# A decode attention and FFN kernel on one Trainium2 core: tiles of four KV heads in 32 KB runs, expanded scores with an additive mask, full-tile transposes of the probabilities, FFN and output weights loaded last

## The chip, the cores and the metric

The kernel runs on one core of one Trainium2 chip (trn2). The metric is the device time of one execution in microseconds (us), as the median of several. Every place in time named below ("190.3 us") is a place in a profile, counted from the start of its span.

The engines are PE (matmul), DVE (vector), ACT (scalar), POOL (GpSimd) and SP, which here only issues transfers. The data moves on 16 DMA engines. A run counts as slow when it is over 1.5% above the fastest of the same kernel.

## The reference

Four decode tokens, one in each of four batches, go through grouped-query attention over the last 4096 places of a KV cache, and through a gated FFN. A scalar gate mixes the two results.

```python
# B = 4, D = 512, Hq = 32 query heads, Hkv = 8 KV heads, Dh = 128, F = 1792, window W = 4096; all bf16
g = sigmoid((x * gate_w).sum(-1, keepdims=True))
q = (x @ wq).reshape(B, 1, 32, 128).transpose(0, 2, 1, 3)
k, v = k_cache[:, :, -W:, :], v_cache[:, :, -W:, :]      # each KV head serves 4 query heads
p = softmax(q @ k.T * Dh ** -0.5)
a = (p @ v).reshape(B, 1, 4096) @ wo
b = (relu(x @ W_gate) * (x @ W_up)) @ W_down
out = g * a + (1 - g) * b                                # [4, 1, 512]
```

The K window and the V window are 33.6 MB each, wq and wo 4.2 MB each, the three FFN matrices 1.8 MB each: 81 MB, and each byte is read once.

## The kernel before

It works on "pairs": two KV heads of one batch, 2 MB of K and 2 MB of V. Two pairs make a set; there are eight sets, and a set is scored together. The names in the code are those of the steps:

- `KT`: K comes in with rows on the partitions (16 KB runs in HBM). PE transposes it as fp32 words that hold two bf16 each, and DVE and ACT copy the result back from PSUM, the memory that PE writes its results to.
- `SC`: scores. Each head has 8 rows in a group of 32 partitions, so 32 of 128 partitions of a score tile carry data. `SW` shares the maxima between partitions.
- `EXP`: two exponentials a set, of 64 partitions each, write the even and the odd columns of `pe`.
- `PT`: PE multiplies `pe` with a selection matrix, which gives transposed probabilities. `PV`: 64 small matmuls a pair apply V. `NORM` divides by the row sums (`RS`), `OQ` rearranges the result for the output matmul.
- `GU`, `HT`, `FFN`, `T2`: the FFN. `WO`: the 32 matmuls with wo. `FIN`: the mix.

```python
KSLOTS, VSLOTS = 4, 5            # slots of 2 MB; gate, up and down weights pass through V slots 2, 3, 4
VLAG, VPIECES = 3, 4             # Wbig (4 MB) holds wq first, then wo
...
def _dma_order():
    o = [("k", 0), ("x",), ("gw",), ("wq",), ("k", 1), ("wg",), ("k", 2), ("wu",), ("k", 3), ("wd",), ("v", 0)]
    for i in range(4, NPAIR):
        o += [("k", i), ("v", i - VLAG)] if i < NPAIR - 1 else [("v", i - VLAG)]
        if i == 4:
            o.append(("wo",))
        if i == NPAIR - 2:
            o[-1:] = [("k", NPAIR - 1)] + o[-1:]
    o += [("v", i) for i in range(NPAIR - VLAG, NPAIR)]
    return o
...
def _pe_order():                 # its end, after the scores of the last set
    ...
    i = NPAIR - 4
    o += [("OQ", i), ("PV", i + 1), ("PT", NSET - 1), ("OQ", i + 1), ("RS", NSET - 1), ("PV", i + 2), ("OQ", i + 2)]
    o += [("WO", 1), ("PV", i + 3), ("OQ", i + 3), ("WO", 2)]
...
# SC: 8 rows a head, two matmuls (e) for the two interleaved halves of Dh
mm(bk[32 * j:32 * j + 8, :], qblk[:, g, 8 * e:8 * e + 8], rhs, e == 0, e == 1, ..., pos=(0, 32 * j))
...
# EXP, for n in range(2)
a.activation(pev[r, :, n], sc[r, :], ACTF.Exp, bias=negmax[r, ...], scale=SCALE, accum_out=rowsum[r, ...])
...
# PT: 32 matmuls a set
mm(banks[tr(key)][:, 32 * q:32 * q + 32], pe[:, 128 * c:128 * c + 128], sel[:, :], True, True, ...)
...
# PV: 64 matmuls a pair, 128 a set
mm(banks[OB][r:r + 8, 0:128], pT[:, s % 2, c0:c0 + 8], Vsb[:, i % VSLOTS, 128 * ch:128 * ch + 128], ...)
```

The weights come early in this order, and the last four loads are V tiles. So everything from the last scores to the end of the output matmul has to be done around or after the last landing.

## Time and profile before

| | before |
|---|---|
| time, median (range) | 209.43 us (208.85 to 210.42, 3 runs) |
| span of the profile | 209.7 us |
| last K tile landed | 171.66 us |
| 16 DMA engines done, first / last | 192.94 / 197.80 us |
| last landing to end of span | 11.9 us |

The landings are not on the page; they are the completion updates in the trace, of which each load of a tile or of weights has 16, one from each DMA engine. The Trainium skill ("DMA: Bandwidth & Descriptors", section "Why a DMA increments its semaphore by 16 and not by 1") states this, and the updates here agree: a load has landed with the last of its 16.

From the page of the kernel before: the span; busy time, share of the span and number of instructions of each engine; the mean busy share of the DMA engines in tenths, in 40 slices of 5.2 us; the packets, MB and share of 16 engines of the queue that carries PE's instructions; and the group of the exponentials (busy us, mean ns, idle time before them and what ended it).

```profile
span 209.7 us, 5539 instructions
...
PE 145.5 (69%) x2527; PEld 114.8 (55%) x2527; DVE 121.5 (58%) x284; ACT 69.7 (33%) x62; POOL 4.5 (2%) x20
...
DMA  5999999999999999999999999999999999998200
...
q8 instruction: 19, 0.31, 0.6%
...
L677 ACT ACTIVATE pe<-sc,negmax 64x2048 bf16<-64x2048 bf16 x16 | 41.7, 2604 | 42.3 <-DVE negmax L603 42.1
```

No compute engine is above 69%, and the DMA engines are at nine tenths from slice 2 to slice 36. The kernel is bound by its loads up to the last landing. The two slices of 0 at the end are another matter: there nothing is loaded, and the span still runs. (The page counts 19 instruction packets in the span; one more is in the trace.)

The timeline of the kernel before, at its end. Columns: start, length in us, engine, line, operation, tiles and shapes, number, and in brackets the idle time before it and what ended that.

```profile
178.34 3.75 PE L337 MATMUL bank<-unmix,Ksb 128*128 128x128 f32 x32
...
188.22 2.57 ACT L677 ACTIVATE pe<-sc,negmax 64x2048 bf16<-64x2048 bf16 x1 [5.55 <-DVE negmax L603]
...
190.87 2.57 ACT L677 ACTIVATE pe<-sc,negmax 64x2048 bf16<-64x2048 bf16 x1
...
193.53 1.03 PE L333 MATMUL bank<-sel,pe 128*128 128x32 bf16 x32 [1.39 <-ACT pe L677]
...
199.23 2.72 PE L333 MATMUL bank<-Wbig,oq 128*4 128x512 bf16 x6 [0.33 <-DVE oq L624]
...
202.18 2.08 PE L333 MATMUL bank<-Vsb,pT 128*8 128x128 bf16 x58
...
205.38 1.89 PE L333 MATMUL bank<-Wbig,oq 128*4 128x512 bf16 x8 [0.33 <-DVE oq L624]
...
207.31 0.74 DVE L640 SCALAR_TENSOR_TENSOR osum<-bank,gg,t 4x512 bf16<-4x512 f32 x1 [1.98 <-PE bank L333]
```

The tail read in order: the last K tile landed at 171.66, but PE transposes it only at 178.34, behind the tile before it. Then come the scores, the two exponentials one after the other (188.22 to 193.44), the transposed probabilities, `PV` with `NORM` and `OQ` between, and the last 16 output matmuls, which end at 207.3.

Four windows of the kernel before. Columns: window, length, then busy us (and number) of PE, PEld, DVE, ACT and POOL, granted PE clock (1.00 is the full clock, 0.50 half of it), DMA share, GB/s.

```profile
68.00:70.00 2.00, 0.00 (x0) 0.00 (x0) 0.00 (x0) 0.00 (x0) 0.00 (x0) 0.50 1.04 416
...
190.00:192.00 2.00, 1.19 (x42) 1.05 (x41) 0.00 (x0) 1.97 (x3) 0.00 (x0) 0.55 0.96 387
200.00:202.00 2.00, 2.00 (x12) 0.64 (x11) 0.00 (x0) 0.00 (x0) 0.00 (x0) 0.50 0.00 0
204.00:206.00 2.00, 1.20 (x30) 0.57 (x22) 0.53 (x2) 0.00 (x0) 0.00 (x0) 1.00 0.00 0
```

In the first window PE waits for data and its clock is at 0.50. The Trainium skill ("TensorE: Matmul & The Clock Gate", section "What's actually happening") says that PE falls to half its clock after an idle window of about 3.4 us. The trace agrees in part: the stretches of its clock record last 3.41 us or a multiple of that. The clock fell at 67.3 us, 2.1 us after PE's last matmul, and at 190.2, when PE had been idle for 1.8 us. In the tail the clock is at half from 190.2 to 203.8 us, so most of the last matmuls run slow.

### The profile page before, as it was taken

How to read it: one execution, taken by the hardware profiler on the slowest of the kernel's cores; microseconds unless marked ns; L12 is line 12 of the kernel's file. 1: busy time of each engine (PE TensorE's matmuls, PEld its weight loads, DVE VectorE, ACT ScalarE, POOL GpSimd, SP SyncE). 2: the span in 40 equal slices, each digit the busy share in tenths (PEclk: the TensorE clock that was granted, in tenths of full speed). 3: DMA queues.
4: the chain of work that ended last, by engine and by line, in shares of the span. 5: the costliest groups of instructions: out<-in, count | busy, mean ns of one | idle time of the engine just before them, and what ended most of it. 6: DMA issues, size and time to landing. Idle time of an engine off the chain costs nothing.

```text
span 209.7 us, 5539 instructions
## 1 busy us (share of the span) xinstructions
PE 145.5 (69%) x2527; PEld 114.8 (55%) x2527; DVE 121.5 (58%) x284; ACT 69.7 (33%) x62; POOL 4.5 (2%) x20
## 2 busy tenths in 40 slices
PE   0385817889784028769876976876749789963794
PEld 0371514667373027559765956763749548842641
DVE  3193676978484005884588586857744729870302
ACT  2000501655090005180527227250903172518000
POOL 7100000000000000000000000000000000000000
PEclk9998888999999557995899697899985999996559
DMA  5999999999999999999999999999999999998200
GB/s 200 432 469 397 409 437 435 413 444 409 431 399 408 443 425 425 428 422 428 425 425 431 419 431 420 425 425 423 422 425 437 416 434 419 434 414 353 80 0 1
DMA packets 6838, 81.35 MB, mean 388 GB/s; under 512 B 792, under 2 KB 800, under 8 KB 2336
## 3 DMA queue, kind: packets, MB, share of 16 engines
q1 hardware_dynamic: 6816, 81.01, 91.7%
q8 instruction: 19, 0.31, 0.6%
q14 instruction: 3, 0.02, 0.0%
HBM read 81.01 MB, written 0.00 MB: 386 GB/s over the span
## 4 chain that ended last, share of the span: by engine, by line
DMA 40%; PE 34%; DVE 13%; ACT 8%; SPq 3%; issue 2%; ACTq 0%; DVEq 0%
DMA Ksb<-in_A_k_cache_dram 32%; PE bank L333 21%; PE bank L337 13%; DMA Wbig<-in_A_wq_dram 8%; ACT pe L677 8%; DVE Ksb L545 5%; DVE sc L592 3%; SPq L258 3%; DVE pe L582 2%; DVE qblk L574 1%; DVE osum L640 0%; DVE osb L617 0%; DVE rowmax L596 0%; DVE hmax L601 0%; DVE negmax L603 0%
## 5 line engine op out<-in xcount | busy, mean ns | idle before, releaser
L337 PE MATMUL bank<-unmix,Ksb 128*128 128x128 f32 x512 | 73.3, 309 | 31.6 <-DMA Ksb<-in_A_k_cache_dram 26.7
L545 DVE COPY Ksb<-bank 128x1024 bf16<-128x1024 bf16 x104 | 66.6, 685 | 43.0 <-PE bank L337 41.8
L337 PEld LDWEIGHTS bank<-unmix,Ksb 128*128 128x128 f32 x512 | 67.5, 162 | 36.0 <-issue 17.8
L677 ACT ACTIVATE pe<-sc,negmax 64x2048 bf16<-64x2048 bf16 x16 | 41.7, 2604 | 42.3 <-DVE negmax L603 42.1
L654 ACT ACTIVATE Ksb<-bank 128x1024 bf16<-128x1024 bf16 x24 | 24.2, 1023 | 61.9 <-PE bank L337 61.9
L333 PE MATMUL bank<-Vsb,pT 128*8 128x128 bf16 x1024 | 22.3, 243 | 2.6 <-issue 2.6
L592 DVE TENSOR_SCALAR_CACHE_REDUCE sc<-bank 128x512 bf16<-128x512 f32 x32 | 20.8, 688 | 5.2 <-PE bank L333 4.7
L333 PE MATMUL bank<-Ksb,qblk 128*8 128x512 bf16 x256 | 18.5, 389 | 5.1 <-DVE Ksb L545 4.7
L333 PEld LDWEIGHTS bank<-Vsb,pT 128*8 128x8 bf16 x1024 | 18.2, 95 | 4.0 <-issue 3.9
L617 DVE TENSOR_SCALAR osb<-bank,recip 128x128 bf16<-128x128 f32 x16 | 5.6, 351 | 18.2 <-PE bank L333 18.2
L333 PE MATMUL bank<-sel,pe 128*128 128x32 bf16 x256 | 7.9, 178 | 7.8 <-ACT pe L677 5.7
L608 DVE CAST pT<-bank 128x512 bf16<-128x512 f32 x16 | 10.3, 684 | 3.6 <-PE bank L333 3.6
L333 PEld LDWEIGHTS bank<-Ksb,qblk 128*8 128x8 bf16 x256 | 6.2, 84 | 11.1 <-DVE Ksb L545 6.1
L333 PEld LDWEIGHTS bank<-sel,pe 128*128 128x128 bf16 x256 | 7.1, 97 | 8.9 <-DVE oq L624 3.9
L333 PE MATMUL bank<-Wbig,oq 128*4 128x512 bf16 x32 | 9.1, 440 | 0.7 <-DVE oq L624 0.7
L333 PEld LDWEIGHTS bank<-rowmax,perm 128*128 128x128 bf16 x8 | 0.8, 96 | 13.4 <-DVE rowmax L596 13.4
L333 PE MATMUL bank<-rowmax,perm 128*128 128x1 bf16 x8 | 1.4, 178 | 9.2 <-DVE rowmax L596 9.2
L333 PEld LDWEIGHTS bank<-oneh,osb 128*32 128x32 bf16 x256 | 4.7, 115 | 4.4 <-DVE osb L617 1.5
L333 PE MATMUL bank<-oneh,osb 128*32 128x2 bf16 x256 | 5.5, 176 | 1.2 <-DVE osb L617 1.0
L333 PE MATMUL bank<-rowsum,wsum 128*128 128x1 f32 x32 | 5.7, 283 | 0.0
L333 PEld LDWEIGHTS bank<-Wbig,oq 128*4 128x4 bf16 x32 | 2.7, 92 | 5.3 <-issue 1.8
L333 PEld LDWEIGHTS bank<-rowsum,wsum 128*128 128x128 f32 x32 | 5.2, 231 | 0.1
(59 smaller groups left out, 50.9 us busy)
## 6 DMA issues: line engine op xcount, KB each, us to landing
Ksb<-in_A_k_cache_dram SPq DMA_DIRECT2D x16, 2048.0 KB, 26.7
Vsb<-in_A_v_cache_dram SPq DMA_DIRECT2D x15, 2048.0 KB, 33.5
Wbig<-in_A_wq_dram SPq DMA_DIRECT2D x1, 4096.0 KB, 15.9
Wbig<-in_A_wo_dram SPq DMA_DIRECT2D x1, 4096.0 KB, 33.7
Vsb<-in_A_v_cache_dram SPq DMA_DIRECT2D x4, 512.0 KB, 28.5
Vsb<-in_B_W_gate_dram SPq DMA_DIRECT2D x1, 1792.0 KB, 23.7
Vsb<-in_B_W_up_dram SPq DMA_DIRECT2D x1, 1792.0 KB, 33.1
Vsb<-in_B_W_down_dram SPq DMA_DIRECT2D x1, 1792.0 KB, 41.0
```

The costliest lines, as they stand in the source:

```text
L258: E.op(lambda: e.dma_start(dst, src), ev=ev, waits=waits, ctr=ctr)
L333: E.op(lambda: t.matmul(out_, lhsT, rhs, start=start, stop=stop, tile_position=pos, skip_group_check=True), ev=ev, waits=waits)
L337: E.op(lambda: t.transpose(out_, in_, idn), ev=ev, waits=waits)
L545: E.op(lambda: v.tensor_copy(kt_dst(i, f), bankb[tr(key)]), ev=("E",) + key, waits=[key])
L574: E.op(lambda r=r, u=u, b=b: v.tensor_copy(qv[r, b, n, :, :, :, u], src[r, :, :, b, :]), ev=("E",) + key if lastop else None, waits=[key, ...
L582: E.op(lambda n=n: v.memset(pev[64 * n:64 * n + 64, :, 1 - n], 0.0), ev=("PEZ",) if n else None, waits=[("QT", 1)])
L592: E.op(lambda: v.tensor_scalar(sc[:, 512 * f:512 * f + 512], banks[scb(key)], 1.0, None, op0=ALU.mult, op1=ALU.max, accum_out=mx4[:, f:f + ...
L608: E.op(lambda: v.tensor_copy(pT[:, s % 2, 512 * f:512 * f + 512], banks[tr(key)]), ev=("E",) + key, waits=[key] + ([("PV", 2 * s - 3)] if ...
L617: E.op(lambda: v.tensor_scalar(osb[:, i % 2, :], banks[OB][:, 0:128], recip[:, i % 4:i % 4 + 1], None, op0=ALU.mult), ev=("NORM", i), wait ...
L654: E.op(lambda: a.activation(kt_dst(i, f), bankb[tr(key)], ACTF.Copy), ev=("E",) + key, waits=[key])
L677: E.op(lambda r=r, n=n: a.activation(pev[r, :, n], sc[r, :], ACTF.Exp, bias=negmax[r, s % 2:s % 2 + 1], scale=SCALE, accum_out=rowsum[r, s ...
```

## The change: its intent, and the diff

The kernel is rewritten around tiles of four KV heads: a set is one K tile and one V tile of 4 MB, in runs of 32 KB. The scores are "expanded" to all 128 partitions: every row is scored against the columns of all four heads, and a mask matmul adds −1e30 where the column belongs to another head, so that the exponential makes it 0. So one exponential of 128 partitions does a set, the transposes of `pe` are plain 128 by 128 ones, and `PV` has 64 matmuls a set instead of 128. wq, K, V, gate/up and wo share a ring of five 4 MB slots. Gate and up are loaded before the last V tile, down after it, and wo last in five pieces, so that little compute stands after the last landing. Six of the 16 K copies of a set go to ACT, before three of 16.

The diff, cut to its core:

```diff
-KSLOTS = 4
-VSLOTS = 5
-VLAG = 3
-VPIECES = 4
+NSLOT = 5
+WO_PIECES = ((0, 16), (16, 24), (24, 28), (28, 30), (30, 32))
...
-    sb("Ksb", [128, KSLOTS, TILE], BF16)
-    sb("Vsb", [128, VSLOTS, TILE], BF16)
-    sb("Wbig", [128, 4, 4096], BF16)
+    sb("slots", [128, NSLOT, 16384], BF16)
+    sb("wdsb", [128, 14 * 512], BF16)
...
 def _pe_order():
-    i = NPAIR - 4
-    o += [("OQ", i), ("PV", i + 1), ("PT", NSET - 1), ("OQ", i + 1), ("RS", NSET - 1), ("PV", i + 2), ("OQ", i + 2)]
-    o += [("WO", 1), ("PV", i + 3), ("OQ", i + 3), ("WO", 2)]
-    return o
+    o = kt(0, 0) + kt(0, 1) + kt(0, 2) + kt(0, 3)
+    o += [("XT",), ("Z",), ("Q",), ("QT",)] + [("SC", 0, f) for f in range(4)] + [("SW", 0)]
+    for s in range(1, NSET):
+        o += kt(s, 0) + [("PT", s - 1), ("RS", s - 1)] + kt(s, 1) + [("SC", s, 0)] + kt(s, 2) + [("SC", s, 1)]
+        o += kt(s, 3) + [("SC", s, 2), ("PV", s - 1), ("SC", s, 3), ("SW", s), ("OQ", s - 1)]
+    s = NSET - 1
+    o += [("PT", s), ("RS", s), ("GU",), ("HT",), ("PV", s), ("OQ", s), ("FFN",)]
+    return o + [("WO", p) for p in range(len(WO_PIECES))]
...
 def _dma_order():
-    o = [("k", 0), ("x",), ("gw",), ("wq",), ("k", 1), ("wg",), ("k", 2), ("wu",), ("k", 3), ("wd",), ("v", 0)]
-    ...
-    o += [("v", i) for i in range(NPAIR - VLAG, NPAIR)]
-    return o
+    o = [("k", 0), ("x",), ("gw",), ("wq",), ("k", 1), ("v", 0)]
     for s in range(2, NSET):
+        o += [("k", s), ("v", s - 1)]
+    return o + [("wg",), ("wu",), ("v", NSET - 1), ("wd",)] + [("wo", p) for p in range(len(WO_PIECES))]
...
-def _kt_on_act(i, f):
-    return i % 2 == 1 and f in (1, 3, 6)
+def _kt_on_act(g):
+    return g in (1, 4, 6, 9, 12, 14)
...
         def SC(s, f):
+            for e in range(3):
+                for c in range(4):
+                    rows = bk[32 * c:32 * c + 32, :]
+                    ck = 16 * f + 4 * c
+                    lhsT, rhs = (R["maskl"][:, :], R["maskr"][:, :]) if e == 2 else (qblk[:, s, e, :], kt[:, ck:ck + 4, :, e])
+                    mm(rows, lhsT, rhs, e == 0, e == 2, ev=key if (e, c) == (2, 3) else None, ..., pos=(0, 32 * c))
...
         def PT(s):
-                for q in range(16):
-                    mm(banks[tr(key)][:, 32 * q:32 * q + 32], pe[:, 128 * c:128 * c + 128], sel[:, :], True, True, ...)
+                for q in range(8):
+                    tp(bankb[tr(key)][:, 128 * q:128 * q + 128], pe[:, 128 * c:128 * c + 128], identb[:, :], ...)
...
         def EXP(s):
-            for n in range(2):
-                E.op(lambda r=r, n=n: a.activation(pev[r, :, n], sc[r, :], ACTF.Exp, ...), ev=("EXP", s, n), waits=w)
+            E.op(lambda: a.activation(pe[:, :], sc[:, :], ACTF.Exp, ...), ev=("EXP", s), waits=w)
```

## The prediction

> **What bounds the kernel now.** The DMA engines. The page's 40-slice row shows DMA at 9 tenths from slice 2 to slice 37, at about 425 GB/s, while PE is busy 69%, DVE 58% and ACT 33%. 81.0 MB at that rate is about 191 us. The queue starts at 2.2 us, and the last V piece lands at 197.8 us (the trace's completion updates). The other 12 us are a tail in which nothing is loaded.
>
> That tail is compute which the load order puts last. The last K tile lands at 171.7 us, but PE reaches its transposes only at 178; then scores, max, two exponentials (188.2 to 193.5 in the timeline), probability transposes, three PV with NORM and OQ between, and 16 output matmuls, ending at 207.3. PE has half its clock from 190.3 to 203.6 (windows view).
>
> **DMA after the change.** Bytes are the same. The packet records show 613 ns for 16 KB, 1213 for 32 KB, 161 for 4 KB: about 13 ns of fixed cost each. With 32 KB runs for K and V, each engine saves about 2 us. Engine skew matters more: the first engine ends at 192.9, the last at 197.8. A tile has landed only when all 16 engines have posted (the Trainium skill, "DMA: Bandwidth & Descriptors", section "Why a DMA increments its semaphore by 16 and not by 1"; the updates agree). The skew grows in steps of about 1.5 us, which I read as 16 KB instruction fetches (20 in the run) sharing an engine. PE falls from 2527 to about 1810 matmuls; I estimate 14 fetches and 1 to 2 us less skew. Last landing: 193 to 195.5 us. Slot waits should not bite: a tile has some 39 us (four loads of 9.7 us) to be used up.
>
> **Compute.** Two half-partition exponentials of 2.6 us become one full one per set: ACT saves about 21 us there, but takes 48 instead of 24 K copies (1.02 us each); DVE loses those 24 (0.685 us each). Mask matmuls add half to the score matmuls, about 1 us a set. PE needs 15 to 17 us a set against 19.5 us of loading. All this is off the critical path; compute should wait for K at every set.
>
> **The new tail.** K7 lands near 151 us and is used up by about 171, gate and up follow, V7 lands near 180. PV7 (2 us warm, 3.7 at half clock), NORM, OQ to about 185; 14 FFN matmuls (0.23 us warm, 0.43 cold) to 188 to 190; T2 0.74; 32 output matmuls (0.24 us warm: 7.6 us) to 196.5 to 199; then FIN, store and end, 2.4 us in the trace. PE idles from about 172 to 180, so it starts cold: the skill ("TensorE: Matmul & The Clock Gate", section "What's actually happening") says one idle window of about 3.4 us halves the clock; the trace agrees (0.50 after the idle stretch at 66 us, and after 190). So the tail is PE-bound by 1 to 3 us.
>
> **Predicted: 200 us, 197 to 203.5 (8 in 10); faster by over 2% 0.93, within 2% 0.05, slower 0.02.**
>
> **Right if:** DMA stays at 9 tenths to about 193 us; instruction packets drop to about 14; exponentials are 8 of 2 to 2.6 us; from the last landing to the end is 4 to 8 us, mostly output matmuls.
> **Wrong if:** PE or DVE needs over 19.5 us a set, so that slot waits open gaps in the DMA row; 32 KB runs over four heads read slower; the clock stays at half through all output matmuls (about +4 us); or instruction fetches fall on one engine.

## The result, and the profile after

| | before | after |
|---|---|---|
| time, median (range) | 209.8 us (208.85 to 210.42, 4 runs) | 202.07 us (201.06 to 202.7, 4 runs) |
| span of the profile | 209.7 us | 199.3 us |
| DMA engines done, first / last | 192.94 / 197.80 us | 191.25 / 194.73 us |
| last landing to end of span | 11.9 us | 4.6 us |

The ratio is 0.9642, with a 95% interval from 0.9589 to 0.9694: the change is faster. Ratios, here and below, are worked out from the fast runs of the same rounds; they are not quite the ratio of the medians or means quoted (202.0 over 209.7 is 0.963). Outputs were correct in all runs.

The spans differ by 10.4 us and the times by 7.7 us. The profile of before is a long execution, and that of after is the fastest of its four. The four spans of after are 199.3, 199.8, 200.9 and 201.0 us.

The page of the kernel after, the lines that answer to those of before:

```profile
span 199.3 us, 4082 instructions
...
PE 145.7 (73%) x1806; PEld 110.9 (56%) x1806; DVE 104.7 (53%) x244; ACT 67.6 (34%) x70; POOL 13.2 (7%) x38
...
DMA  5999999999999999999999999999999999999960
...
q8 instruction: 14, 0.23, 0.5%
...
L618 ACT ACTIVATE pe<-sc,negmax 128x2048 bf16<-128x2048 bf16 x8 | 16.0, 2001 | 37.9 <-DVE negmax L547 37.9
```

PE is as busy as before with 721 fewer matmuls, since the larger ones take longer. The exponentials fell from 41.7 to 16.0 us, and ACT's total hardly moved, since it took 24 K copies of about 1.02 us from DVE. The DMA row has nines to slice 38 and one slice of 0 in place of two.

The waits of the kernel after (engine, line, what it waited for: us in all, times, longest):

```profile
PE bank L321 <- DMA slots<-in_A_k_cache_dram: 31.4, 8, 13.3
```

PE waits for K in each of the eight sets: compute is ahead of the loads all the way.

The timeline of the kernel after, from the last K tile on:

```profile
152.72 3.28 PE L321 MATMUL bank<-identf,slots 128*128 128x128 f32 x16 [2.83 <-DMA slots<-in_A_k_cache_dram]
...
169.69 2.00 ACT L618 ACTIVATE pe<-sc,negmax 128x2048 bf16<-128x2048 bf16 x1 [4.40 <-DVE negmax L547]
...
180.59 3.52 PE L317 MATMUL bank<-slots,pT 128*32 128x256 bf16 x64 [1.66 <-DMA slots<-in_A_v_cache_dram]
...
185.14 3.18 PE L317 MATMUL bank<-wdsb,hT 128*4 128x512 bf16 x14
...
189.80 7.07 PE L317 MATMUL bank<-slots,oq 128*4 128x512 bf16 x32 [1.48 <-DMA slots<-in_A_wo_dram]
...
196.90 0.74 DVE L583 SCALAR_TENSOR_TENSOR osum<-bank,gg,t 4x512 bf16<-4x512 f32 x1 [7.81 <-PE bank L317]
...
197.67 0.29 SPq L276 DMA_DIRECT2D out_dram<-osum  x1
```

The last exponential is done by 171.7 us (by 193.4 in the kernel before). What is left after the loads is one block of 32 output matmuls. It starts when the first piece of wo (half of its rows) lands at 189.75, and takes 7.07 us. The later pieces land at 192.25, 193.46, 194.10 and 194.73, ahead of the matmuls that use them.

Windows of the kernel after, columns as above:

```profile
182.00:184.00 2.00, 2.00 (x44) 1.28 (x33) 0.00 (x0) 0.00 (x0) 0.00 (x0) 0.53 1.03 436
186.00:188.00 2.00, 2.00 (x11) 0.76 (x9) 0.00 (x0) 0.00 (x0) 0.00 (x0) 1.00 0.98 410
...
194.00:196.00 2.00, 2.00 (x11) 0.77 (x9) 0.00 (x0) 0.00 (x0) 0.00 (x0) 1.00 0.03 10
```

`PV` of the last set still runs near half clock, and the FFN and output matmuls run at full clock.

The last load's 16 completion updates show the rest of the gain:

```
before  192.94 193.03 193.04 193.12 193.13 193.29 193.75 194.89 196.03 196.06 196.06 196.13 196.16 196.20 197.70 197.80
after   191.25 191.29 191.44 191.62 191.95 191.95 192.00 192.61 192.96 193.38 194.49 194.52 194.54 194.63 194.72 194.73
```

The first engine is done 1.69 us earlier, the last 3.07 us. The last landing of after hardly moves: in eight profiles, two of it and six of variants with the same tiles, the same runs of K and V, no more instruction packets and the weights last, it lies between 194.68 and 195.16.

### The profile page after: what moved, and what is told of

Same layout as the page of the kernel before. It is cut to its first block, busy times and chain, and to the rows that moved or that the text cites. A ratio compares the mean times of both kernels' runs of the same rounds, so it can differ in the third digit from the quotient of the medians.

```text
span 199.3 us, 4082 instructions
## 1 busy us (share of the span) xinstructions
PE 145.7 (73%) x1806; PEld 110.9 (56%) x1806; DVE 104.7 (53%) x244; ACT 67.6 (34%) x70; POOL 13.2 (7%) x38
## 4 chain that ended last, share of the span: by engine, by line
DMA 73%; PE 21%; DVE 2%; SPq 2%; issue 0%
DMA slots<-in_A_k_cache_dram 43%; DMA slots<-in_A_wo_dram 20%; DMA slots<-in_A_wq_dram 11%; PE bank L321 10%; PE bank L317 10%; SPq L250 2%; DVE qblk L525 1%; DVE osum L583 0%; DVE sc L535 0%; DVE pe L510 0%; DVE pe L512 0%; DVE gp L515 0%
## 5 line engine op out<-in xcount | busy, mean ns | idle before, releaser
L321 PE MATMUL bank<-identf,slots 128*128 128x128 f32 x512 | 73.2, 304 | 31.4 <-DMA slots<-in_A_k_cache_dram 31.4
L321 PEld LDWEIGHTS bank<-identf,slots 128*128 128x128 f32 x512 | 65.5, 159 | 39.3 <-DMA slots<-in_A_k_cache_dram 32.1
L503 DVE COPY slots<-bank 128x1024 bf16<-128x1024 bf16 x80 | 54.3, 690 | 51.0 <-PE bank L321 49.4
L596 ACT ACTIVATE slots<-bank 128x1024 bf16<-128x1024 bf16 x48 | 47.8, 1022 | 63.6 <-PE bank L321 63.4
L618 ACT ACTIVATE pe<-sc,negmax 128x2048 bf16<-128x2048 bf16 x8 | 16.0, 2001 | 37.9 <-DVE negmax L547 37.9
L317 PE MATMUL bank<-slots,qblk 128*32 128x512 bf16 x256 | 20.5, 394 | 1.3 <-DVE qblk L525 1.2
L317 PE MATMUL bank<-slots,pT 128*32 128x256 bf16 x512 | 17.0, 290 | 1.7 <-DMA slots<-in_A_v_cache_dram 1.7
L317 PEld LDWEIGHTS bank<-slots,pT 128*32 128x32 bf16 x512 | 14.5, 102 | 4.2 <-DMA slots<-in_A_v_cache_dram 1.7
L321 PE MATMUL bank<-identb,pe 128*128 128x128 bf16 x128 | 11.6, 261 | 2.2 <-ACT pe L618 2.2
L553 DVE COPY pT<-bank 128x1024 bf16<-128x1024 bf16 x16 | 10.6, 686 | 3.9 <-PE bank L321 3.8
L317 PE MATMUL bank<-maskr,maskl 128*32 128x512 bf16 x128 | 12.5, 378 | 0.0
```

Of the source, the lines that this page charges most:

```text
L317: E.op(lambda: t.matmul(out_, lhsT, rhs, start=start, stop=stop, tile_position=pos, skip_group_check=True), ev=ev, waits=waits)
L321: E.op(lambda: t.transpose(out_, in_, idn), ev=ev, waits=waits)
L503: E.op(lambda: v.tensor_copy(kt_dst(s, g), bankb[tr(key)]), ev=("E",) + key, waits=[key])
L553: E.op(lambda: v.tensor_copy(dst, bankb[tr(key)]), ev=("E",) + key, waits=[key] + ([("PV", s - 2)] if s >= 2 else []))
L596: E.op(lambda: a.activation(kt_dst(s, g), bankb[tr(key)], ACTF.Copy), ev=("E",) + key, waits=[key])
L618: E.op(lambda: a.activation(pe[:, :], sc[:, :], ACTF.Exp, bias=negmax[:, s % 2:s % 2 + 1], scale=SCALE, accum_out=rowsum[:, s % 2:s % 2 + ...
```

## The experiments

Two theories stand against each other. By the first, the gain has two parts: the new load order takes compute out of the tail, and larger runs and fewer instruction packets make the last landing earlier; the cheaper compute is off the critical path. By the rival, the cheaper compute (one exponential, fewer matmuls, copies moved to ACT) brings the gain. A later question is what bounds the tail that is left: the landing of wo or the clock of PE. Mean for the kernel after: 202.0 us, both in the four runs above and in six more (run `after_again`).

### The old kernel with the new load order: before_last

The kernel before keeps its pairs, its scores and its exponentials. Only the order of the loads and of what uses them is that of after, with wo in five pieces; gate, up and down pass through slots of K for that.

```diff
-VLAG = 3
+VLAG = 2
+WO_PIECES = ((0, 16), (16, 24), (24, 28), (28, 30), (30, 32))
...
-    o = [("k", 0), ("x",), ("gw",), ("wq",), ("k", 1), ("wg",), ("k", 2), ("wu",), ("k", 3), ("wd",), ("v", 0)]
+    o = [("k", 0), ("x",), ("gw",), ("wq",), ("k", 1), ("k", 2), ("k", 3), ("v", 0), ("v", 1)]
...
-    o += [("v", i) for i in range(NPAIR - VLAG, NPAIR)]
-    return o
+    o += [("wg",), ("wu",), ("v", NPAIR - 2), ("v", NPAIR - 1), ("wd",)]
+    return o + [("wo", p) for p in range(len(WO_PIECES))]
...
-    o += [("WO", 1), ("PV", i + 3), ("OQ", i + 3), ("WO", 2)]
+    o += [("PV", i + 3), ("OQ", i + 3), ("FFN",)]
+    return o + [("WO", p) for p in range(len(WO_PIECES))]
```

> The kernel before with nothing changed but the load order: FFN and output weights last, gate, up and down into freed K slots, the output weights in five pieces, all 32 output matmuls at the end. If the load order makes the gain: wo's first piece lands near 192.7 us (5 us before a last landing of about 197.8), 7 us of output matmuls follow it, so the time falls by about 7 us, to 202 to 204. If the new tiles, the single exponential and the smaller PE program make it, this stays within 2 us of before, 208 to 210.

Measured: 204.76 us (204.15 to 206.16), ratio 0.9789 (0.9692 to 0.9886), called unclear because the interval spans the 2% line. The mean is 204.95 us, against 209.2 us for before in the same rounds, so 4.3 us come from the order alone (the time is a little above the range that I expected, the gain still over half of the 7.7 us). From the timeline of this run:

```profile
192.97 7.07 PE L331 MATMUL bank<-Wbig,oq 128*4 128x512 bf16 x32 [1.91 <-DMA Wbig<-in_A_wo_dram]
```

The tail is that of after: the same block of 7.07 us, started by the landing of the first piece of wo, with 16 half-partition exponentials and 2 MB tiles elsewhere. The last landing is still at 197.94 us with 20 instruction packets for PE, as in before. What after has beyond this run is 3.2 us of earlier landing (194.73) and 3.0 us of time. This speaks against the rival.

### The new kernel with the old load order: old_order

The kernel after, with the weights early, wo pinned in the slot of wq, and the last V tile last in four pieces.

```diff
-    o = [("k", 0), ("x",), ("gw",), ("wq",), ("k", 1), ("v", 0)]
+    o = [("k", 0), ("x",), ("gw",), ("wq",), ("k", 1), ("wg",), ("wu",), ("wd",), ("v", 0)]
     for s in range(2, NSET):
-        o += [("k", s), ("v", s - 1)]
-    return o + [("wg",), ("wu",), ("v", NSET - 1), ("wd",)] + [("wo", p) for p in range(len(WO_PIECES))]
+        o += [("k", s), ("v", s - 1)] + ([("wo", p) for p in range(len(WO_PIECES))] if s == 2 else [])
+    return o + [("v", NSET - 1, p) for p in range(4)]
...
-        n = turn % NSLOT
+        n = turn % (NSLOT - 1)
```

> The kernel after with its compute and tiles, but with the old load order: FFN and output weights early, the last V tile last, in four pieces. If the load order makes the gain: the last piece of V lands near 195 us, then a PV piece, NORM, OQ and 32 output matmuls (7 us warm, 13 at half clock) still stand behind it, so 208 to 214 us, all of the gain lost or more. If tiles and compute make the gain: under 204 us.

Measured: 212.59 us (211.96 to 213.37), ratio 1.0156 (1.0068 to 1.0244): slower than before, as expected. Its timeline at the end:

```profile
197.00 3.61 PE L327 MATMUL bank<-slots,pT 128*32 128x256 bf16 x64
...
202.10 7.07 PE L327 MATMUL bank<-slots,oq 128*4 128x512 bf16 x32 [0.42 <-DVE oq L581]
```

The last landing is at 195.33, but the last K tile landed at 175.75, and the critical chain of the trace is compute from there on. The cheaper compute is all there, and the kernel is slower than before. Moreover, in the new layout each output matmul takes rows of heads of every set, so none can start before the last set is done, and all 32 stand at the end; before could do 16 of them early. (This run has four slots for the tiles instead of five, since wo occupies one; that part is not separated. So the run shows that the cheaper compute is not enough, and not by itself what the order is worth.)

### Runs of 16 KB: runs16k

Each 4 MB tile of K and V is loaded by two transfers, in runs of 16 KB.

```diff
-                load((k.upper(), it[1]), f"d_{k}{it[1] % 3}", slot(*it), src.rearrange("h (r c) d -> r h (c d)", r=32),
-                     waits=w)
+                src = src.rearrange("h (r c) d -> r h (c d)", r=32)
+                for p in range(2):
+                    load((k.upper(), it[1], p), f"d_{k}{it[1] % 3}", slot(*it)[:, 8192 * p:8192 * p + 8192],
+                         src[:, :, 8192 * p:8192 * p + 8192], waits=w)
```

> The kernel after with each K and V tile loaded by two transfers of 16 KB runs instead of one of 32 KB runs. If the run length counts at about 13 ns a packet: 128 more packets an engine, +1.7 us on every engine's end, the last landing near 196.4 us and the time up by 1.5 to 2 us. If run length is of no account: under 0.5 us.

Measured: 203.61 us (202.21 to 204.15), ratio 0.9707 (0.959 to 0.9824); the mean is 203.4 us, 1.4 us above after. The first engine is done at 192.39 us (1.14 later than in after) and the last landing is at 196.09 (1.36 later), still with 14 instruction packets. So the 32 KB runs are worth 1.1 to 1.4 us against this profile of after, and 0.9 to 1.4 us if the last landings of the eight profiles above are taken. With 128 more packets on each engine 1.1 to 1.4 us is about 9 to 11 ns a packet; the prediction used 13.

### More instruction fetches, on POOL: fetch

3072 tiny memsets on POOL, which has nothing to do after the first 20 us, were meant to add instruction packets and nothing else.

```diff
+    sb("junk", [128, 3072], BF16)
...
+        for n in range(3072):
+            E.op(lambda n=n: e.memset(R["junk"][:, n:n + 1], 0.0))
```

> The kernel after with 3072 tiny memsets on POOL, which is idle: 12 more 16 KB of program to fetch. If instruction fetches make the engines' skew: about 26 instruction packets instead of 14, the last landing 1.5 to 3 us later (196 to 197.5 us) and the time up by as much, with no engine's compute changed. If the skew has another cause: last landing and time unchanged within 0.5 us.

Measured: 215.56 us (214.63 to 217.25), ratio 1.0305 (1.0188 to 1.0422). The sign is as expected; the size is not, 13.7 us in place of a few. From the page of this run:

```profile
DMA  5989999999999999999999999999999999993000
...
q14 instruction: 29, 0.23, 0.3%
...
L314 POOL MEMSET junk<- 128x1 bf16 x3072 | 102.8, 102 | 28.7 <-issue 28.7
```

The completion updates of the last load tell where the 13.7 us are:

```
fetch   191.33 191.56 191.69 191.91 192.28 192.31 193.37 193.41 193.55 193.66 194.39 194.64 195.06 195.19 195.31 208.33
```

Fifteen engines end about as in after (at most 0.6 us later), and one at 208.33. The additional packets of POOL (queue 14, 8 KB each; 24 more in the trace while the loads run, the page counts one more) have no engine in the records. But since only one engine is late, they must have gone through that one: (208.33 − 194.73) / 24 = 0.57 us for a packet. A load has landed only when its slowest engine has, so a single engine stretched the kernel.

### The control, a busy POOL without fetches: pool_busy

64 large memsets keep POOL busy with 64 instructions.

```diff
+        for n in range(64):
+            op(lambda: e.memset(R["junk"][:, :], 0.0), ("JUNK", n))
```

> The control of fetch: POOL as idle otherwise, kept busy for some 100 us by 64 large memsets instead of 3072 tiny ones, so the same load of an idle engine with next to no program to fetch. If fetch was slow for its instruction packets: within 0.7 us of the kernel after, last landing near 194.7 us. If it was slow because POOL's memsets disturb the other engines or SBUF: several us slower, as fetch was.

From the page of this run, POOL's instruction packets and the group of the memsets:

```profile
q14 instruction: 4, 0.03, 0.0%
...
L314 POOL MEMSET junk<- 128x3072 bf16 x64 | 170.2, 2659 | 3.7
```

Measured: 202.24 us (201.03 to 203.14), ratio 0.9628 (0.9527 to 0.9728), the time of after; the last landing is at 194.87. The memsets ran longer than I had estimated (170 us), which makes the control stronger. What slowed `fetch` is not a busy POOL, but its instruction packets.

### More instruction fetches, on PE: pe_fetch

1540 tiny matmuls, 110 behind each of seven sets, bring PE's instruction packets back to 20 in the kernel after.

```diff
-        o += kt(s, 3) + [("SC", s, 2), ("PV", s - 1), ("SC", s, 3), ("SW", s), ("OQ", s - 1)]
+        o += kt(s, 3) + [("SC", s, 2), ("PV", s - 1), ("SC", s, 3), ("SW", s), ("OQ", s - 1), ("JUNK", 110)]
...
+        def JUNK(n):
+            for _ in range(n):
+                mm(banks[ACC][0:4, 0:1], xT[:, 0:4], R["maskr"][:, 0:1], True, True, waits=[("GE",)])
```

> The kernel after with 110 tiny matmuls of no use after each of seven sets, in the stretch in which PE waits for K: 1540 more PE instructions, so that PE has as many to fetch as in the kernel before, 20 packets of 16 KB instead of 14. Without a change the last landing was 194.7 to 194.9 us in five profiles. If PE's instruction packets make the engines' skew: the last landing 1 to 2 us later, 195.8 to 196.8 us, spread over several engines, and the time 1 to 2 us longer, 203 to 204 us. If only POOL's do: last landing below 195.1 us, time within 0.7 us of 202 us.

PE's instruction packets on its page:

```profile
q8 instruction: 20, 0.33, 0.6%
```

The completion updates of its last load:

```
pe_fetch 191.18 191.41 191.50 191.56 191.69 192.14 192.15 193.54 194.50 194.55 194.59 194.74 195.85 195.97 196.07 196.10
```

The first engine ends as in after (191.18, against 191.25), so the loads had no gaps; the last landing is 1.37 us later, at 196.10. The mean of the 16 ends rises by 0.59 us: 16 × 0.59 / 6 is 1.58 us of one DMA engine for each packet. That is with one profile of after; with `after_again`, `warm`, `copies_dve` and `pool_busy` in its place it is 1.1 to 1.4 us, and the records of the packets themselves last 1.06 us here (median). So a packet costs 1.1 to 1.6 us, which fits the steps of 1.1 to 1.5 us in the updates of before.

All six additional packets fall into the time of the loads here: the last of the 20 starts at 189.1 us. In before two of its 20 start after the last landing, at 198.1 and 210.7 us. So the change took four packets out of the time of the loads (18 before, 14 after), and not six.

The time is 204.26 us (203.53 to 206.25), ratio 0.9751 (0.9688 to 0.9813), 2.4 us above after in the mean. That is more than the landing: in this profile PE also stalled for 1.03 us within `PV` and ran the FFN at half clock (4.87 us), so this run is evidence for the landing and not for the exact time.

### All K copies on DVE: copies_dve

```diff
 def _kt_on_act(g):
-    return g in (1, 4, 6, 9, 12, 14)
+    return False
```

> The kernel after with all 16 K copies of a set on DVE instead of 10 there and 6 on ACT. By the means of the profile DVE then needs some 17 us a set against 19.4 us of loading. If compute between the loads is off the critical path: within 0.7 us of the kernel after, 201.3 to 202.7 us, though a quarter of its K copies moved. If the split of the copies is part of the gain: 3 us slower or more.

The group of the copies on the page of this run:

```profile
L503 DVE COPY slots<-bank 128x1024 bf16<-128x1024 bf16 x128 | 80.7, 682 | 32.4 <-PE bank L321 32.1
```

Measured: 202.19 us (201.26 to 203.19), ratio 0.9643 (0.9559 to 0.9728): no change. DVE has 128.4 us of work instead of 104.7 and ACT 19.9 instead of 67.6 (48 of the 128 copies moved, not the quarter of the expectation). So the split of the copies, and the 24 copies moved to ACT by the change, are off the critical path.

### wo in one transfer: wo_one

```diff
-WO_PIECES = ((0, 16), (16, 24), (24, 28), (28, 30), (30, 32))
+WO_PIECES = ((0, 32),)
```

> The kernel after with the output weights loaded by one transfer instead of five. All 32 output matmuls then start after the last landing, near 194.6 us, 5 us later than now: 206 to 207 us if they run at the full clock (7 us), up to 210 if PE has fallen to half by then. If the pieces do nothing: 202 us.

The output matmuls in the timeline of this run:

```profile
195.07 8.51 PE L317 MATMUL bank<-slots,oq 128*4 128x512 bf16 x32 [6.26 <-DMA slots<-in_A_wo_dram]
```

Measured: 207.94 us (207.8 to 208.71), ratio 0.9924 (0.985 to 0.9998). The load lands at 195.03, as late as the last piece in after, and all 32 matmuls come behind it; PE waited for 6.26 us, its clock fell to half from 191.2 to 198.0, and the block took 8.51 us. The pieces are worth about 6 us, most of what the change gains. So it is not enough that wo comes last: it has to come in pieces.

### The clock: after_again, warm

`after_again` is the kernel after, unchanged, in the rounds of the next three. `warm` adds 22 matmuls without use around `PT`, `GU` and `HT`, to keep PE's clock up until the last `PV`.

```diff
-    o += [("PT", s), ("RS", s), ("GU",), ("HT",), ("PV", s), ("OQ", s), ("FFN",)]
+    o += [("JUNK", 10), ("PT", s), ("RS", s), ("GU",), ("JUNK", 4), ("HT",), ("JUNK", 8), ("PV", s), ("OQ", s), ("FFN",)]
...
+        def JUNK(n):
+            for _ in range(n):
+                mm(banks[ACC][0:4, :], xT[:, 0:4], R["maskr"][:, :], True, True)
```

> The kernel after, unchanged, as the yardstick for the other runs of this chip: 201 to 202.7 us, ratio near 0.964.

> The kernel after with 22 matmuls of no use in PE's idle stretches after the last scores, so that the last PV and the FFN matmuls run at the full clock. If the first 16 output matmuls wait for their piece of weights (which landed at 189.75 us in the profile of after, with PE idle from 188.3), nothing is gained in the runs with a high mean clock and at most 1 to 1.5 us in the others: 200.5 to 202 us. If the cold clock sets the tail: 2 to 4 us faster than the kernel after.

Measured: `after_again` 202.03 us (201.1 to 203.25), ratio 0.9616 (0.9567 to 0.9665); `warm` 201.16 us (201.02 to 202.01), ratio 0.9583 (0.954 to 0.9626). The profile of `after_again` fell on another phase of the clock than that of after. Its timeline:

```profile
184.82 4.87 PE L317 MATMUL bank<-wdsb,hT 128*4 128x512 bf16 x14 [1.13 <-DMA wdsb<-in_B_W_down_dram]
...
190.61 7.07 PE L317 MATMUL bank<-slots,oq 128*4 128x512 bf16 x32 [0.93 <-DVE t L579]
```

And one window of it, columns as above:

```profile
186.00:188.00 2.00, 2.00 (x7) 0.58 (x5) 0.00 (x0) 0.00 (x0) 0.00 (x0) 0.50 0.98 410
```

Here the FFN takes 4.87 us in place of 3.18, and the output matmuls wait for its result (`T2`, the 0.93 us of DVE) and not for wo, which had landed at 189.68. Its span is 200.1 us, against 199.3. So in these two profiles the same kernel ends in two ways, 0.8 us apart, by the phase of the clock. (The ten spans of after reach from 199.3 to 201.5 us; the rest of that scatter is not explained here.) The skill ("TensorE: Matmul & The Clock Gate", section "What's actually happening") says that the window is free-running, so that the number of slow matmuls varies from run to run; these two profiles agree. In the profile of `warm` the clock stays at full from 156.0 us until after the last matmul (FFN 3.18 us, the block started at 190.00 by the landing at 189.95), though PE still waits 2.54 us for the last V tile; the mean of `warm` is 0.7 us below that of after.

### Smaller pieces: finer, finer_warm

`finer` loads the last V tile before gate and up, splits wo into seven pieces of which the first has 8 of the 32 rows, and gives the output its own PSUM bank, so that it need not wait for `T2`. `finer_warm` is the same with 36 useless matmuls.

```diff
-WO_PIECES = ((0, 16), (16, 24), (24, 28), (28, 30), (30, 32))
+WO_PIECES = ((0, 8), (8, 16), (16, 20), (20, 24), (24, 28), (28, 30), (30, 32))
...
-    o += [("PT", s), ("RS", s), ("GU",), ("HT",), ("PV", s), ("OQ", s), ("FFN",)]
+    o += [("PT", s), ("RS", s), ("PV", s), ("OQ", s), ("GU",), ("HT",), ("FFN",)]
...
-    return o + [("wg",), ("wu",), ("v", NSET - 1), ("wd",)] + [("wo", p) for p in range(len(WO_PIECES))]
+    return o + [("v", NSET - 1), ("wg",), ("wu",), ("wd",)] + [("wo", p) for p in range(len(WO_PIECES))]
...
-            w = [("WO", p), ("T2",)] + [("E", "OQ", s) for s in range(NSET)]
+            w = [("WO", p)] + [("E", "OQ", s) for s in range(NSET)]
...
-                mm(banks[ACC][0:4, :], oq[:, i, :], Wo[:, i, :], i == 0, i == 31, ...)
+                mm(banks[OB][0:4, :], oq[:, i, :], Wo[:, i, :], i == 0, i == 31, ...)
```

> The kernel after with V7 loaded before the gate and up weights, the output weights in seven pieces beginning with 8 rows instead of 16, and the output matmuls in a bank of their own, so that they no longer wait for T2. If the end is set by the 16-row first piece and the 7 us of matmuls that follow it: the matmuls start near 188 us, keep up with the pieces and end within 1 us of the last landing, so 1 to 1.5 us faster than the kernel after. If the end is set by the last landing alone, or PE falls back to half clock: no change within 0.5 us, or slower.

> finer with 36 matmuls of no use to hold the clock at full speed from the last scores to the output matmuls. 0.5 us or more faster than finer, and with less spread between its runs, if half clock in some runs delays FFN and the first output matmuls; the same as finer if the landings alone set the end.

`finer` measured 201.41 us (200.86 to 202.1), ratio 0.9588 (0.9544 to 0.9632): 0.6 us below after, where I had expected 1 to 1.5. Its timeline says why:

```profile
185.27 5.33 PE L317 MATMUL bank<-wdsb,hT 128*4 128x512 bf16 x14 [0.93 <-DMA wdsb<-in_B_W_down_dram]
...
190.43 7.07 PE L317 MATMUL bank<-slots,oq 128*4 128x512 bf16 x32
```

PE is now busy without a gap to the end, and it is slow: the FFN took 5.33 us at half clock, and the gain of the earlier first piece went into it. `finer_warm` measured 199.8 us (199.59 to 199.98), ratio 0.9507 (0.9463 to 0.9551). Its timeline:

```profile
185.15 3.18 PE L317 MATMUL bank<-wdsb,hT 128*4 128x512 bf16 x14
...
188.17 7.61 PE L317 MATMUL bank<-slots,oq 128*4 128x512 bf16 x32
```

The output matmuls begin 1.6 us earlier than in after and end at 195.78, 0.65 us behind the last landing at 195.13. In this version the end hangs on the landings: the critical chain of the trace is loads up to a piece of wo that landed at 193.85, then the last 8 output matmuls. It beats both kernels, after by 2.2 us, and scatters by only 0.4 us over six runs. Neither half does this alone: the changes of `finer`, which were not tested one by one, gave 0.6, the warm clock 0.7.

## Why the prediction was right or wrong

| step | predicted | measured |
|---|---|---|
| last landing | 193 to 195.5 us | 194.73 |
| instruction packets of PE | about 14 | 14 |
| gain of 32 KB runs | about 2 us an engine | 1.14 us, and 1.36 in the last landing |
| last `PV` | 3.7 us at half clock | 3.52 (1.93 in `after_again`) |
| end of the output matmuls | 196.5 to 199 us | 196.88 |
| exponentials | 8 of 2 to 2.6 us | 8 of 2.00 |
| last landing to end of span | 4 to 8 us | 4.6 |
| time | 200.0 us (197 to 203.5) | 202.07 |

The prediction was right in sign, size and its main mechanism, and the measured time lies in its range, 2 us above the middle.

**Where the gain is.** Take the mean time, 209.7 us before and 202.0 after. A last landing at 194.73 in place of 197.80 gives 3.1 us of the 7.7. The rest, about 4.6 us, is a shorter tail, which the load order gives: `before_last` got 4.3 us of it without any of the new compute, and missed just the earlier landing. These are differences between runs, each good to about half a us.

**The earlier landing.** 32 KB runs (1.36 us) and instruction packets of PE (1.37 us for six) were each tested by putting them back, in one profile each. Of the packets only four were in the time of the loads; by proportion (an estimate) they are worth 0.9 us. If the two add up, which no run tests, they explain 2.3 to 2.7 of the 3.1 us. The remaining 0.4 to 0.8 us was not tested. It may be the 4 KB runs of wo and of the last V tile in before, which after no longer has in such number. The prediction's reading of the 1.5 us steps as instruction fetches was a guess when it was written, and it counted two packets that come after the loads; `pe_fetch` bears the reading out.

**Compute off the path.** `copies_dve` and `old_order` show it from two sides: 24 us more on DVE cost nothing, and all the cheaper compute with the old order (and one slot fewer) is slower than before. The tile layout is still needed in an indirect way, because it brings the long runs and the fewer instructions.

**The mis-sized terms.** The first two account for the 2 us; in the third the number was right by luck.

- The sum was done in spans. The predicted end, 200 us, is the end of a span, and the four spans of after are 199.3 to 201.0 us, 200.25 in the mean. A time is 1.75 us longer. The span of the profile before (209.7) happened to equal the median time (209.43), since that profile shows a long execution; so the two looked like the same thing. Two numbers that agree by accident hid a term.
- "So the tail is PE-bound by 1 to 3 us" and "14 FFN matmuls (0.23 us warm, 0.43 cold)" were both half right. In the profile of after the output matmuls wait 1.48 us for the first piece of wo, so a landing sets their start; from there PE works without a gap and ends 2.1 us behind the last landing. In that of `after_again` the FFN is slow (4.87 us, 0.35 each), and PE and `T2` set the start. The difference is 0.8 us.
- "PE idles from about 172 to 180, so it starts cold" did not happen. In after PE was busy for 6.1 of these 8 us; its clock rose at 177.1 and fell at 180.5, after 1.6 us of idle time, just before the last `PV`. In `after_again` that `PV` ran at full clock. So the 3.7 us of the prediction met the 3.52 us of this one profile by luck.

The gain of the 32 KB runs was put at 2 us and is about 1.1 to 1.4. The skew between first and last engine, put at 1 to 2 us less, fell by 1.38 us (4.86 to 3.48). The mask matmuls were put at 1 us a set; the page of after has 12.5 us for them, 1.6 a set, which is off the path.

**The fears.** No slot wait opened a gap in the DMA row; 32 KB runs are not slower; the clock did not stay at half through the output matmuls. That instruction fetches might fall on one engine did not happen in the change, but `fetch` shows that for POOL they do, and what it costs.

## What to carry to other kernels

When a kernel is bound by its loads, choose what is loaded last by how little compute must follow it, and split that load so that the compute begins with its first piece; making off-path compute cheaper gained nothing here. Read the skew between the DMA engines, not only their mean rate: the slowest engine sets the landing, and the instruction fetches of a long program are packets on those engines too. Before adding up a predicted time, check from several runs how a span and a time differ, and whether the profile at hand shows a usual execution.

## What the Trainium skill lacked or had wrong

- "Runtime: NRT & Kernel Launch", section "Instruction fetch mechanics", calls the cost of crossing a block of instructions mostly hidden. In this kernel, which is bound by its loads, it is not: a 16 KB packet of PE's instructions costs 1.1 to 1.6 us of one DMA engine, and six of them moved the last landing by 1.37 us (`pe_fetch`).
- The same section says that instructions are refilled in blocks of 16 KB. PE's packets are of 16 KB here; POOL's are of 8 KB, and with some 24 more of them one DMA engine alone was late (13.6 us in the last landing of `fetch`, 0.57 us a packet). The section says nothing of how the fetches are spread over the engines.
- "DMA: Bandwidth & Descriptors", section "Where 436 GB/s comes from", says that the HBM side, about 358 GB/s for a core, limits transfers from HBM to SBUF. With one core at work this kernel kept about 425 GB/s for some 190 us. The measurement of 425 GB/s for 16 MB on the same page (section "Measured (HBM→SBUF, 128 partitions, SWDGE, issued from GpSimd)") fits, and beside it the page names the condition that this sentence leaves out: about 358 GB/s is the share of a core when both cores of the pair are loading, which no run here tests.
- No page that I found gives the time of a packet by its length for loads issued by SP. Medians in these traces: 84 ns for 2 KB, 159 to 161 for 4 KB, 312 for 8 KB, 613 for 16 KB, 1213 for 32 KB.
- "TensorE: Matmul & The Clock Gate", section "What's actually happening", gives half clock after an idle window and full clock after a busy one, and does not say how busy or idle a window must be. In the kernel before the clock stayed at half from 190.2 to 203.8 us, although PE was busy for 10.6 of those 13.6 us. And a window that is only partly idle was enough to lose it: at 190.2 us PE had been idle for 1.8 us, in after at 180.5 for 1.6 us.
